# Threshold attention and a bilinear FFN on one core: FFN columns spread over the slots up to the next block, product with v moved by 0.4 of a slot

## The chip, the core and the metric

The kernel runs on one core of a Trainium2 chip. The metric is the device time of one execution in microseconds (us); the kernel before has a median of 1560.83 us over three executions (1559.90, 1560.83 and 1564.76). Everything is in fp32.

## What is computed

Eight batches of eight heads, 576 rows of 64 values each, go through an attention whose weights are kept only where a score is within tau of the maximum of its row. The result, as 4608 tokens of 512 values, goes through a bilinear FFN with 1536 inner columns.

```python
scores = scale * np.matmul(q, k.transpose(0, 1, 3, 2))
thresh = np.max(scores, axis=-1, keepdims=True) - tau
scores = np.where(scores >= thresh, scores, -1000000000.0)
attn = np.exp(scores - np.max(scores, axis=-1, keepdims=True))
attn = attn / (np.sum(attn, axis=-1, keepdims=True) + 1e-09)
attn_out = np.matmul(attn, v)            # (8, 8, 576, 64)
x = attn_out.transpose(0, 2, 1, 3).reshape(4608, 512)
out = ((x @ w_a) * (x @ w_b)) @ w_out    # w_a, w_b: 512 x 1536, w_out: 1536 x 512
```

## The kernel before

**Units and slots.** Two heads of a batch make a pair; there are 32 pairs, four to a batch. The 576 query rows of a pair are cut into four tiles of 128 rows (u = 0 to 3) and a tail of 64 (u = 4, `NT`). A pair and a u are a *unit*, 160 in all. For each batch come first the units u = 0 and 1 of its four pairs, then u = 2, 3 and the tail of each pair (the first batch has an order of its own). The main loop (L632) takes one unit per turn; such a turn, g = 0 to 162, is called a *slot* here. A slot begins on PE with the score matmuls of its unit.

**What a slot issues, in this order.** The program is emitted in one pass, and `keep_order` (L710) fixes on every engine the order in which the instructions were emitted. So where a line stands in the loop decides where its instructions stand in each engine's queue. A slot of the steady part does this:

1. `scores(i, u)` (L640): eight score matmuls into two PSUM buffers `sc` (one for a tail); on DVE a maximum per buffer (L319), on POOL the bias and the threshold (L320, L321).
2. `turn_back` (L641): on SP the load of `wT`, the transposed weights of an earlier unit, out of a scratch tensor `swap` in DRAM; `exchange_blocks` (L642): on POOL eight copies xS<-xT for a block that has become complete.
3. `turn_blocks` of the previous unit (L656): on DVE its transposes (L401, L416), on SP the stores into `swap`.
4. `advance(PORTIONS[0] * pace)` (L658): the first share of the slot's FFN work.
5. `weigh(i, u)` (L660): on ACT the exponential of each `sc` buffer (L332), on DVE the comparison with the threshold (L336), which reads the same `sc` buffer and is its last reader.
6. `prep` (L668): on DVE the transposes of q and k of the next pair; k of a pair is transposed in the slot just before its first scores.
7. `advance(PORTIONS[1] * pace)`, then reciprocal (DVE) and `normalise` (ACT, L355), loads on SP, `advance(PORTIONS[2] * pace)`.
8. If the unit n = g - 3 (`PV_LAG`) completes a part of its pair: `make_room`, then `weighted` (L703), the product with v.
9. `advance(PORTIONS[3] * pace)`.

In the first 15 slots ACT, DVE and POOL also convert the weights of the FFN piece by piece, and the first eight units are turned on PE instead of through DRAM.

**The product with v.** `weighted` (L483) calls `product` (L441), 18 matmuls into one PSUM buffer `pv`, over 256 columns, or over 320 where a part takes in the pair's tail (64 alone for the tails of the first batch). `join` (L437) then adds the two halves of `pv`: a copy of one half on ACT (L438), an addition of the other on DVE (L439); with a tail a second copy and a second addition follow. When the fourth pair of a batch has its part, a *block* of 256 tokens is complete and waits for the FFN.

**The FFN.** `ffn` (L505) is a generator. It works on a block in steps of PE columns: for each of six slices of the inner columns 2048 columns with `w_a` into a PSUM buffer `pab` (emptied by ACT, L536) and 2048 with `w_b` (emptied by DVE, L538), then twice 6144 columns with `w_out` into `po`. A block is 36,864 columns; there are 18 blocks. `advance(cols)` (L575) runs the generator until `cols` columns are used up; when no block is there it returns at once. `make_room` (L596) runs it on until the open PSUM buffer has had at least 1024 columns and has at least 1024 left. `pace`, set at the head of a slot, is 0.09 of a block, plus 576 columns for the product with v, plus 0.05 of what the backlog has above one block; a product takes its columns (5 x 256 or 5 x 320) off what is owed.

**PSUM.** Scores, `pab`, `po` and `pv` share four buffers (`banks`, L122). A buffer is free for the next tile when the last reader of its former tile has been emitted, and the first matmul into it waits for that reader.

After the last slot the remaining blocks run alone (L707).

Of the kernel before, what the change touches and what calls it, by code (L numbers as in the profile page):

```python
# [19 lines left out]
def float_of(bits):  # L20
    return struct.unpack("<f", struct.pack("<I", bits))[0]

PV_LAG = 3
BY_PE = 8
XT_BUFS = 7
W_BUFS = 4
# [3 lines left out]
PACE = 0.09  # L30
CATCH_UP = 0.05
PACE_EARLY = 0.04
ROOM = 1024
PORTIONS = (0.3, 0.4, 0.1, 0.2)


def keep_order(tc):
# [13 lines left out]
def kernel(  # L51
# [37 lines left out]
    B, H, S, D = q.shape  # L89
# [4 lines left out]
    HP = H // 2  # L94
    NT = 4
# [10 lines left out]
    NSLOT = 9  # L106
# [193 lines left out]
    def prep_copy(mT, tp):  # L300
        nc.vector.tensor_copy(mT.rearrange("p (c k) -> p c k", c=2), tp)  # L301
# [82 lines left out]
    def part(i, u):  # L384

        if i < HP:
            return {1: (i, 0), 3: (i, 1), NT: (i, 2)}.get(u)
        return {1: (i, 0), NT: (i, 1)}.get(u)

    def width(i, h):  # L390
        return (HALF, HALF, TAIL)[h] if i < HP else (HALF, HALF + TAIL)[h]
# [45 lines left out]
    def join(out, lo, hi):  # L437
        nc.scalar.copy(out, lo)  # L438
        nc.vector.tensor_tensor(out, out, hi, op=ALU.add)  # L439

    def product(wT, vm, n):  # L441

        pv = banks(n, "pv")
        for s in (NT, 0, 1, 2, 3):
            for r in range(2):
                rows = slice(r * D, (r + 1) * D)
                for j in ((r,) if s == NT else range(2)):
                    k0 = NT if s == NT else 5 * j + s
                    nc.tensor.matmul(pv[j * D:(j + 1) * D, r], vm[rows, k0], wT[rows, k0],  # L449
                                     start=(s == (NT if j == r else 0)), stop=(s == NT - 1))  # L450
        return pv

    def x_tile(name):
        return work.tile([P, HP, HALF], FP32, tag="xT", bufs=XT_BUFS, name=name)

    def exchange(x, xs, hp, c0, c1, engine):

        for r in range(2):
            engine.tensor_copy(xs[r * D:(r + 1) * D, hp, c0:c1], x[(1 - r) * D:(2 - r) * D, hp, c0:c1])  # L459

    def exchange_blocks():
        while complete:
            x, what = complete.pop(0)
            xs = x_tile("xS")
            for hp in range(HP):
                exchange(x, xs, hp, 0, HALF, nc.gpsimd)
            blocks.append(((x, xs), what))
# [15 lines left out]
    def weighted(i, h):  # L483

        b, hp = pairs[i]
        n = width(i, h)
        pv = product(turned.pop((i, h)), loaded[i]["v"], n)
        if h < 2:
            if hp == 0:
                x_of[b, h] = x_tile("xT")  # L490
            lo, hi = (pv[:, r, 0:HALF].rearrange("p (i t e) -> p i t e", t=2, e=Q) for r in range(2))
            join(x_of[b, h][:, hp, :].rearrange("p (t i e) -> p i t e", t=2, e=Q), lo, hi)
            if hp == HP - 1:
                complete.append((x_of.pop((b, h)), ("half", b, h)))
        if n % HALF:
            t = b % GT
            if hp == 0 and t == 0:
                xtail_of[b // GT] = x_tile("xt")
            join(xtail_of[b // GT][:, hp, t * TAIL:(t + 1) * TAIL], pv[:, 0, n - TAIL:n], pv[:, 1, n - TAIL:n])
            del loaded[i], prepared[i]  # L500
            if hp == HP - 1 and t == GT - 1:
                complete.append((xtail_of.pop(b // GT), ("tail", b - t, 0)))
# [69 lines left out]
    BLOCK_COLS = NF * 2 * HP * HALF + 2 * NF * DM  # L572
    running = {"ffn": None, "owed": 0.0, "left": 0, "done": 0, "rest": 0}

    def advance(cols):  # L575
        running["owed"] += cols
        while running["owed"] > 0:
            if running["ffn"] is None:
                if not blocks:
                    running["owed"] = 0.0  # L580
                    return
                running["ffn"] = ffn(*blocks.pop(0))
                running["left"] = BLOCK_COLS
            step, rest = next(running["ffn"], (None, 0))
            if step == 0:
                running["owed"] = 0.0
                return
            if step is None:
                running["ffn"] = None
            else:  # L590
                running["owed"] -= step
                running["left"] -= step
                running["done"] = running["done"] + step if rest else 0
                running["rest"] = rest

    def make_room():  # L596

        while running["rest"] and not (running["done"] >= ROOM and running["rest"] >= ROOM):
            owed = running["owed"]
            running["owed"] = 0.0  # L600
            advance(1)
            running["owed"] += owed - 1

    def backlog():
        return len(blocks) * BLOCK_COLS + (running["left"] if running["ffn"] is not None else 0)
# [3 lines left out]
    units = []  # L609
    for i in range(0, NPR, HP):  # L610
        if i == 0:
            units += [(p, u) for u in (0, 1) for p in range(HP)]
            units += [(p, u) for p in range(HP) for u in (2, 3)]
            units += [(p, NT) for p in range(HP)]
        else:
            units += [(p, u) for p in range(i, i + HP) for u in (0, 1)]
            units += [(p, u) for p in range(i, i + HP) for u in (2, 3, NT)]
    first = {i: g for g, (i, u) in enumerate(units) if u == 0}

    for name in ("q", "k"):  # L620
# [2 lines left out]
    n = 0  # L623
# [4 lines left out]
    def of(g, late):  # L628

        return early.get(g, [])[1:] if late else early.get(g, [])[0:1]  # L630

    for g in range(len(units) + PV_LAG):  # L632
        pace = ((PACE if g > BY_PE else PACE_EARLY) * BLOCK_COLS + (NSLOT + 1) // 2 * S / (NT + 1)
                + CATCH_UP * max(backlog() - BLOCK_COLS, 0))
        written = len(pending)
        here = g < len(units)
        converting = bool(early.get(g)) or bool(early.get(g - 1))
        if here:
            i, u = units[g]
            scores(i, u)  # L640
        turn_back()  # L641
        exchange_blocks()  # L642
        if 2 <= g < BY_PE + 2:
            weighted_unit(*units[g - 2])
            running["owed"] -= (NSLOT + 1) // 2 * P
        for n in of(g - 1, False):
            convert_add(n)
        for n in of(g - 1, True):
            convert_clamp(n)
        if g < 3:  # L650
            prep_copy(*prep_pe(g + 1, "q"))
        for n in of(g - 1, True):
            convert_sign(n)
        load_weights(5 if g < 10 else 4)
        if g > BY_PE and g <= len(units):
            turn_blocks(*units[g - 1])  # L656
        if g > BY_PE:
            advance(PORTIONS[0] * pace)  # L658
        if here:
            weigh(i, u)  # L660
        if 0 < g <= BY_PE:
            turn_pe(*units[g - 1])
        if g < 3:
            prep_copy(*prep_pe(g + 1, "k"))
        for p in range(HP, NPR):
            for name, d in (("q", 2), ("k", 1)):
                if g == first[p] - d:
                    prep(p, name)  # L668
        if g > BY_PE:
            advance(PORTIONS[1] * pace)  # L670
        for n in of(g, False):
            convert_first(n)
            convert_clamp(n)
        if here:
            reciprocal(i, u, nc.scalar if converting else nc.vector)
        for n in of(g - 1, True):
            convert_shift(n)
        for n in of(g - 1, True):
            convert_add(n)
        if here and g < BY_PE:  # L680
            diagonals(i, u)
        elif here:
            normalise(i, u)
        for n in of(g, False):
            convert_sign(n)
        load_weights(5 if g < 10 else 4)
        for p in range(HP, NPR):
            for name, d in (("q", 4), ("k", 3)):
                if g == first[p] - d:
                    load(p, name)  # L690
        for p in range(1, NPR):
            if g == first[p] - 1:
                load_v(p)
        store(written)
        advance((PORTIONS[2] if g > BY_PE else sum(PORTIONS[:3])) * pace)
        for n in of(g, True):
            convert_first(n)
        for n in of(g, False):
            convert_shift(n)
        n = g - PV_LAG  # L700
        if BY_PE <= n < len(units) and part(*units[n]):
            make_room()
            weighted(*part(*units[n]))  # L703
            running["owed"] -= (NSLOT + 1) // 2 * width(*part(*units[n]))
        advance(PORTIONS[3] * pace)
    exchange_blocks()
    while blocks or running["ffn"] is not None:  # L707
# [35 lines left out]
```

## Time and profile before

| what | value |
|---|---|
| median of three executions | 1560.83 us |
| the profiled execution | 1561.63 us |
| its span, first to last instruction | 1559.9 us |
| PE busy | 1490.9 us (96%) |
| DVE busy | 881.9 us (57%) |
| ACT busy | 592.7 us (38%) |
| POOL busy | 260.3 us (17%) |
| mean granted TensorE clock | 0.985 |
| FFN block run alone at the end | 41.4 us `pab` and 20.4 us `po` |

"Busy" is time with an instruction at work; the granted clock is the share of TensorE's pulses that the throttle lets through. In the trace a row "start us, us, engine line op out<-in" is a run of equal instructions; square brackets behind it give the idle time of the engine just before and what ended it. The start of a slot can be read from the first `sc` matmul of its unit: slot 9 begins at 95.3 us, slot 16 at 160.8, slot 30 at 270.4, slot 42 at 366.2, slot 63 at 536.5 and slot 158 at 1354.5.

### The profile page before, as it was taken

Reading aid. Unit: us, or ns where it says so; the run is one execution under the profiler, and the core shown is the slowest. Engines: PE = TensorE matmul, PEld = TensorE weight load, DVE = VectorE, ACT = ScalarE, POOL = GpSimd, SP = SyncE. Lnnn points to the kernel's source line nnn. Section 1 sums busy time; section 2 is a strip of 40 time slices with the busy share of each in tenths; the row PEclk is TensorE's granted clock in tenths of the full one; section 3 lists DMA queues with packets and bytes.
Section 4 is the critical chain, followed back from the end, with each engine's and each line's share of the span. In section 5 each row is a group of like instructions: output and inputs, shape, how many; then the busy total and the mean of one; then the engine's idle time right before and its main releaser. Section 6 shows DMA issues by size and latency. Waiting matters only on the chain.

```text
span 1559.9 us, 51105 instructions
## 1 busy us (share of the span) xinstructions
PE 1490.9 (96%) x22640; PEld 1087.8 (70%) x22640; DVE 881.9 (57%) x1844; ACT 592.7 (38%) x935; POOL 260.3 (17%) x662
## 2 busy tenths in 40 slices
PE   5779999898999999999999999999999999999998
PEld 3666585674768777677867686867686768586775
DVE  5999576465656665675544755466555765510010
ACT  4767344343434443443332443243433443310000
POOL 2666211111111111121100101011110111010000
PEclk8889999998999999999999999999999999999999
DMA  9648887679767886687455965588657976530000
GB/s 202 147 139 225 179 159 166 141 151 193 158 141 169 175 194 142 157 171 179 101 128 117 187 151 140 114 174 180 150 130 140 186 160 140 130 85 16 2 15 15
DMA packets 624558, 220.38 MB, mean 141 GB/s; under 512 B 542929, under 2 KB 612049, under 8 KB 624337
## 3 DMA queue, kind: packets, MB, share of 16 engines
q1 hardware_dynamic: 621968, 216.52, 63.4%
q8 instruction: 178, 2.92, 0.8%
q10 hardware_dynamic: 2368, 0.59, 0.2%
q14 instruction: 44, 0.35, 0.1%
HBM read 127.40 MB, written 89.65 MB: 139 GB/s over the span
## 4 chain that ended last, share of the span: by engine, by line
PE 77%; DVE 8%; DMA 5%; SPq 3%; ACT 2%; issue 2%; POOL 0%; DVEq 0%; POOLq 0%; ACTq 0%
PE pab L530 42%; PE po L550 19%; PE pv L449 8%; PE sc L312 8%; SPq L411 2%; DVE w L336 2%; DMA wT<-swap 2%; DVE mx L319 2%; DMA swap<-tb 2%; DVE low L226 1%; DVE tb L401 1%; SPq L140 1%; DMA qm<-in_q_dram 1%; SPq L423 0%; DMA raw<-in_moe_w_b_dram 0%
## 5 line engine op out<-in xcount | busy, mean ns | idle before, releaser
L550 PE MATMUL po<-wo_sb,h 64*64 64x512 f32 x3456 | 410.1, 590 | 0.0
L332 ACT ACTIVATE w<-sc,bias,scalars 128x576 f32<-128x576 f32 x288 | 228.6, 829 | 237.1 <-POOL bias L320 233.8
L550 PEld LDWEIGHTS po<-wo_sb,h 64*64 64x64 f32 x3456 | 178.8, 133 | 178.9 <-issue 166.5
L319 DVE TENSOR_REDUCE mx<-sc 128x1 f32<-128x576 f32 x288 | 205.8, 751 | 163.8 <-PE sc L312 160.1
L355 ACT ACTIVATE w<-w,rcp 128x576 f32<-128x576 f32 x272 | 197.7, 769 | 234.5 <-DVE rcp L349 234.5
L320 POOL TENSOR_SCALAR bias<-mx,scalars 128x1 f32<-128x1 f32 x288 | 84.8, 294 | 1073.5 <-DVE mx L319 1042.9
L530 PE MATMUL pab<-xS,wa_sb 64*64 64x256 f32 (+1 forms) x3520 | 260.2, 377 | 2.4 <-POOL xS L459 2.4
L312 PE MATMUL sc<-kT,qT 64*64 64x288 f32 x2304 | 239.6, 412 | 21.4 <-DVE kT L301 8.1
L530 PE MATMUL pab<-xS,wb_sb 64*64 64x256 f32 (+1 forms) x3520 | 257.3, 375 | 0.0
L336 DVE SCALAR_TENSOR_TENSOR w<-sc,thr,w 128x576 f32<-128x576 f32 x288 | 222.6, 805 | 18.0 <-ACT w L332 13.8
L530 PE MATMUL pab<-xT,wb_sb 64*64 64x256 f32 (+1 forms) x3136 | 224.2, 378 | 3.2 <-DVE h L538 1.6
L530 PE MATMUL pab<-xT,wa_sb 64*64 64x256 f32 (+1 forms) x3136 | 221.8, 373 | 4.9 <-DVE xT L439 3.5
L530 PEld LDWEIGHTS pab<-xS,wa_sb 64*64 64x64 f32 x3520 | 182.2, 134 | 34.9 <-POOL xS L459 9.0
L530 PEld LDWEIGHTS pab<-xS,wb_sb 64*64 64x64 f32 x3520 | 183.7, 134 | 27.2 <-issue 0.3
L449 PE MATMUL pv<-wT,vm 64*64 64x320 f32 (+3 forms) x2592 | 180.4, 389 | 13.9 <-DMA wT<-swap 13.2
L312 PEld LDWEIGHTS sc<-kT,qT 64*64 64x64 f32 x2304 | 137.5, 134 | 71.7 <-issue 26.2
L530 PEld LDWEIGHTS pab<-xT,wa_sb 64*64 64x64 f32 x3136 | 158.6, 133 | 33.0 <-DVE xT L439 3.8
L530 PEld LDWEIGHTS pab<-xT,wb_sb 64*64 64x64 f32 x3136 | 160.4, 136 | 30.4 <-DVE h L538 2.6
L449 PEld LDWEIGHTS pv<-wT,vm 64*64 64x64 f32 x2592 | 129.8, 136 | 59.9 <-issue 24.5
L401 DVE STREAM_TRANSPOSE tb<-w 128x576 f32<-128x576 f32 x240 | 171.2, 751 | 0.0
L538 DVE TENSOR_TENSOR h<-h,pab 128x512 f32<-128x512 f32 (+1 forms) x110 | 72.6, 660 | 139.3 <-PE pab L530 135.7
L439 DVE TENSOR_TENSOR xT<-xT,pv 128x256 f32<-128x256 f32 (+1 forms) x68 | 27.5, 404 | 208.2 <-ACT xT L438 208.2
(59 smaller groups left out, 769.5 us busy)
## 6 DMA issues: line engine op xcount, KB each, us to landing
swap<-tb SPq DMA_DIRECT2D x240, 288.0 KB, 5.1
wT<-swap SPq DMA_DIRECT2D x28, 1440.0 KB, 7.6
wT<-swap SPq DMA_DIRECT2D x32, 1152.0 KB, 6.2
vm<-in_v_dram SPq DMA_DIRECT2D x32, 288.0 KB, 4.2
swap<-tbt SPq DMA_DIRECT2D x128, 72.0 KB, 2.5
out_dram<-osb SPq DMA_DIRECT2D x32, 256.0 KB, 3.8
qm<-in_q_dram SPq DMA_DIRECT2D x112, 72.0 KB, 3.5
km<-in_k_dram SPq DMA_DIRECT2D x112, 72.0 KB, 4.8
```

The source lines that it names most:

```text
L312: nc.tensor.matmul(sc[j if u < NT else 0][to, c], qT[r, q0:q0 + D], kT[r, c * SH:(c + 1) * SH], start=True, stop=True)
L319: nc.vector.tensor_reduce(mx[:, c], sc[j], axis=AX.XY, op=ALU.max)
L320: nc.gpsimd.tensor_scalar(bias[:, c], mx[:, c], e_nscale, None, op0=ALU.mult)
L332: nc.scalar.activation(w.rearrange("p (c k) -> p c k", c=2), s, AF.Exp, bias=bias[:, j:j + 1], scale=e_scale)
L336: nc.vector.scalar_tensor_tensor(out=wv, in0=s, scalar=thr[:, j:j + 1], in1=wv, op0=ALU.is_ge, op1=ALU.mult, accum_out=sums[:, j:j + 1])
L355: nc.scalar.activation(w, w, AF.Copy, scale=rcp[:, j:j + 1])
L401: nc.vector.transpose(tb[:, j * NB:(j + 1) * NB, (u % 2) * Q:(u % 2 + 1) * Q], w.rearrange("p (n e) -> p n e", e=Q))
L411: nc.sync.dma_start(swap[:, :, g * 2 * Q:(g + 1) * 2 * Q].rearrange("c p w -> p c w"), tb[g * Q:(g + 1) * Q])
L449: nc.tensor.matmul(pv[j * D:(j + 1) * D, r], vm[rows, k0], wT[rows, k0], start=(s == (NT if j == r else 0)), stop=(s == NT - 1))
L530: nc.tensor.matmul(pab[c * D:(c + 1) * D, r], w[rows, f // n, k, fs + c * D:fs + (c + 1) * D], moving, start=(k == 0), stop=(k == H - 1))
L538: nc.vector.tensor_tensor(ht, ht, pab, op=ALU.mult)
L550: nc.tensor.matmul(po[c * D:(c + 1) * D, r], ht[rows, t0:t0 + D], wo_sb[rows, F, :], start=(F == 0), stop=(F == NF - 1))
```

## The change

`PV_LAG` goes from 3 to 4, and the product with v moves from the place behind `advance(PORTIONS[2] ...)` to the one behind `advance(PORTIONS[0] ...)`, ahead of `weigh`. Counted in shares of the FFN work it stood at 0.8 of slot n + 3 and stands now at 0.2 of slot n + 4. The shares go from 0.3, 0.4, 0.1, 0.2 to 0.2, 0.4, 0.2, 0.2. `arrivals` lists the slots in which a new block can be begun, and from slot 9 on the pace is no more than the backlog divided by the number of slots up to the next of them. `pace` is worked out behind the scores instead of ahead of them.

```diff
-PV_LAG = 3
+PV_LAG = 4
-PORTIONS = (0.3, 0.4, 0.1, 0.2)
+PORTIONS = (0.2, 0.4, 0.2, 0.2)
...
+    arrivals = [g + PV_LAG + 1 for g, (i, u) in enumerate(units)
+                if i % HP == HP - 1 and part(i, u) and (i >= HP or u == NT - 1)]
...
     for g in range(len(units) + PV_LAG):
-        pace = ((PACE if g > BY_PE else PACE_EARLY) * BLOCK_COLS + (NSLOT + 1) // 2 * S / (NT + 1)
-                + CATCH_UP * max(backlog() - BLOCK_COLS, 0))
...
         turn_back()
         exchange_blocks()
+        pace = (PACE if g > BY_PE else PACE_EARLY) * BLOCK_COLS
+        if g > BY_PE:
+            pace = min(pace, backlog() / (min([a for a in arrivals if a > g] + [len(units) + PV_LAG + 1]) - g))
+        pace += (NSLOT + 1) // 2 * S / (NT + 1) + CATCH_UP * max(backlog() - BLOCK_COLS, 0)
...
         if g > BY_PE:
             advance(PORTIONS[0] * pace)
+            n = g - PV_LAG
+            if BY_PE <= n < len(units) and part(*units[n]):
+                make_room()
+                weighted(*part(*units[n]))
+                running["owed"] -= (NSLOT + 1) // 2 * width(*part(*units[n]))
         if here:
             weigh(i, u)
...
-        n = g - PV_LAG
-        if BY_PE <= n < len(units) and part(*units[n]):
-            make_room()
-            weighted(*part(*units[n]))
-            running["owed"] -= (NSLOT + 1) // 2 * width(*part(*units[n]))
         advance(PORTIONS[3] * pace)
```

No instruction is added or taken away, and none changes its shape; the engines get the same work in another order.

## Prediction

> **What bounds the kernel now.** I read the page first. Its first part gives PE 96% of the span, the second shows where the other 4% lies:
>
> ```profile
> PE 1490.9 (96%) x22640; PEld 1087.8 (70%) x22640; DVE 881.9 (57%) x1844; ACT 592.7 (38%) x935; POOL 260.3 (17%) x662
> PE   5779999898999999999999999999999999999998
> DVE  5999576465656665675544755466555765510010
> PEclk8889999998999999999999999999999999999999
> ```
>
> Each digit is a fortieth of the span, 39 us. From the fifth on PE is the bound; before that DVE is nearly full too. So time is PE's work plus PE's idle time plus what a throttled clock costs. The windows view, cut at slot borders, sizes this:
>
> ```profile
> core 0: us, PE busy (x) PEld busy (x) DVE busy (x) ACT busy (x) POOL busy (x), PEclk, DMA share, GB/s
> 95.28:160.80 65.52, 57.99 (x1043) 41.83 (x1045) 62.56 (x109) 44.71 (x77) 43.50 (x55) 0.95 0.74 196
> 264.80:291.40 26.60, 20.58 (x234) 12.17 (x232) 13.24 (x29) 9.29 (x14) 5.39 (x16) 0.87 0.74 164
> 359.50:389.90 30.40, 22.98 (x241) 12.31 (x237) 17.38 (x39) 12.10 (x18) 5.68 (x17) 0.83 0.94 204
> 420.30:1390.00 969.70, 964.27 (x14697) 713.49 (x14695) 570.73 (x1234) 376.09 (x566) 127.45 (x414) 1.00 0.70 152
> ```
>
> The first line is slots 9 to 15 (weights converted, DVE busy 62.56 of 65.52 us); the next two are the holes; the last, 970 us, has 5.4 us of idle PE. The PE timeline names the holes:
>
> ```profile
> 270.42 1.17 PE L312 MATMUL sc<-kT,qT 64*64 64x288 f32 x8
> 276.70 3.62 PE L449 MATMUL pv<-wT,vm 64*64 64x256 f32 x34 [5.12 <-DMA wT<-swap]
> 366.17 1.46 PE L312 MATMUL sc<-kT,qT 64*64 64x288 f32 x16
> 373.87 5.00 PE L449 MATMUL pv<-wT,vm 64*64 64x320 f32 x34 [6.23 <-DMA wT<-swap]
> ```
>
> In slots 30 and 42 PE has its scores, no FFN column (the backlog is used up) and then waits for the transposed weights. The products behind these waits take 3.62 and 5.00 us where 2.14 is usual for the first form.
>
> **What the skill says.** "TensorE: Matmul & The Clock Gate", Part 1: an idle window of about 3.4 us halves the clock. The trace agrees: mean clocks of 0.87 and 0.83 around the two holes, 1.00 afterwards; idle times of 1.5 us (largest of the 970 us window) leave it at 1.00. "Perfetto Trace Analysis", Per-instruction lifecycle: "ACT/DVE/GPSIMD are strict FIFO", so an instruction that waits holds all behind it. The trace agrees: the rows below keep the order of emission. "PSUM — Partial Sum Buffer", the section on bank collisions: accesses of two engines to a bank must be kept apart by semaphores. The trace agrees: ACT's second copy out of `pv` starts only after DVE's first addition has ended (538.13 after 538.10).
>
> **The change part by part.** Counting the program's instructions on PE, a column of FFN costs (41.42 + 20.41) / 36,864 = 1.68 ns from the block alone at the end; a slot's scores 0.97 us.
>
> *1. The holes go.* In the changed order every slot from 9 on has FFN columns; slots 30 and 42 get 4096 and 3072 instead of none, and the product is 0.4 slot later. Idle PE that goes: 0.88 and 0.29 us (slots 18, 19), 5.12 and 0.90 (30, 31), 6.23 and 1.19 (42, 43): 14.6. Lost pulses: 26.6 x 0.13 + 30.4 x 0.17 = 8.6, of which 1.0 lies in idle time: 7.6. Gain 22.2 us; bounds 20 and 24. What is late next is part 4.
>
> *2. Thinner early slots.* Slots 9 to 15 lose 3072 of 24,064 columns, 5.2 us of PE work. DVE was busy all but 2.96 us there, so they can't get shorter by more. The columns are done later, where PE is full. Cost between 2.2 and 5.2; I take 4.
>
> *3. A block begun as soon as it is there.* In slots 20, 32 and 44 the first `pab` starts with xT and needs xS within 3 us. POOL's eight copies take 3.57 us and stand behind bias and threshold of the slot's scores (3.3 us after its start). Before, this wait cost 0.29, 0.90 and 1.19 us, counted as gone above. Bounds 0 and 6; I take 3.
>
> *4. The product now stands ahead of the exponential.* This is the step that decides. On ACT the copies of `pv` now come before the slot's two exponentials, on DVE the additions before the two comparisons. Queued behind the waiting copy are: exponentials, comparisons, the transposes of k, and, by PSUM, the scores of the next slot. The end of slot 62 and slot 63 of the kernel before give every duration:
>
> ```profile
> 534.24 2.58 PE L449 MATMUL pv<-wT,vm 64*64 64x320 f32 x33
> 537.27 0.37 ACT L438 COPY xT<-pv 128x256 f32<-128x256 f32 x1 [1.60 <-PE pv L449]
> 537.68 0.42 DVE L439 TENSOR_TENSOR xT<-xT,pv 128x256 f32<-128x256 f32 x1 [1.29 <-ACT xT L438]
> 538.13 0.21 ACT L438 COPY xt<-pv 128x64 f32<-128x64 f32 x1 [0.49 <-DVE xT L439]
> ...
> 539.76 1.55 ACT L332 ACTIVATE w<-sc,bias,scalars 128x576 f32<-128x576 f32 x2 [1.41 <-POOL bias L320]
> 541.20 0.78 DVE L336 SCALAR_TENSOR_TENSOR w<-sc,thr,w 128x576 f32<-128x576 f32 x1
> 541.90 0.81 DVE L336 SCALAR_TENSOR_TENSOR w<-sc,thr,w 128x576 f32<-128x576 f32 x1
> 542.64 0.77 DVE L286 STREAM_TRANSPOSE kT<-km 128x576 f32<-128x576 f32 x1
> 543.56 1.20 PE L312 MATMUL sc<-kT,qT 64*64 64x288 f32 x16 [1.07 <-DVE sums L347]
> ```
>
> The last row shows such a wait already: with only 2560 FFN columns in slot 63, the next scores waited 1.07 us. Over all products (medians) ACT is done with `pv` and can start an exponential 2.81 us after a 256-wide product begins and 4.04 us after a 320-wide one; PE itself goes on after 2.03 and 2.6 us. From the exponential's start the first comparison ends at 0.05 + 0.83 + 0.78 = 1.66, with 0.15 to PE (543.41 to 543.56) 1.8 us; the second at 2.6; a transpose of k behind them at 3.3. Until then the next scores can't begin, if they take the buffer of the first score tile (A), of both (B), or need that k (K). The wait is covered only by FFN columns between the product and the end of the slot: for 256 wide and A (2.81 + 1.8 - 2.03) / 1.68 ns = 1531, and so on. Before, the product stood last and the exponentials began 2.5 to 2.8 us into the slot, so A, B and K were ready at 4.6, 5.4 and 6.1 us, under slots of 5.3 to 11 us.
>
> I took the buffers and columns from the order of the built program for the 54 products of slots 25 to 157:
>
> ```
> width, needs  products  columns needed  short of them  their mean columns  missing, us
> 256, none         5          -               0               -                0
> 256, A            9        1531              2             1024               1.7
> 256, B            7        2006              4             1600               2.7
> 256, K            7        2421              6             1877               5.5
> 320, A           10        1923              9             1024              13.6
> 320, B           10        2398              9             1849               8.3
> 320, K            6        2813              6             1109              17.2
> ```
>
> Sum 49 us in 36 slots. One by hand, slot 57: scores 0.97, 1024 columns 1.72, product begins at 2.7; exponential at 6.74, buffer A ready at 8.5; PE has 2.6 for the product and 1280 columns, 7.45: it waits 1.1 us. Since a wait comes every other or third slot and PE is the bound, nothing takes it back. If each release came 0.5 us sooner the 36 short slots would give up 18 us: 31; if 0.25 us later, 58. I take 49.
>
> *5. The product's own start.* In six slots `pv` takes the buffer of a `pab` that ended in this slot, whose multiplication on DVE (0.67 us) now waits behind two maxima and two transposes of 0.75 us, to about 4.9 us. Against PE's own position 0.6 to 1.4 us are missing each time: 6.4 if all hold, 0 if DVE is ahead. I take 3.
>
> *6. The queues.* The product issues no DMA, but frees `wT` (two buffers) and v. For the tails of the first batch, on SP, three loads of `wT` and the load of v for the fifth pair now wait up to half a slot for it; stores into `swap`, output stores and q and k loads stand behind. Their consumers come two slots later, some 14 us, against 6.2 to 7.6 us for the load from issue to landing: 0, at most 2 if this slack were gone. The later place of the pace's arithmetic costs nothing on the chip.
>
> **The sum.** Against the profiled execution's 1561.6 (span 1559.9 and 1.7 around it; 0.8 above the median): 1561.6 - 22.2 + 4 + 3 + 49 + 3 = 1598.4; on the scale of the median 1597.6, so 1598 us.
>
> **Rivals.** (a) *Faster*: the exponential isn't held long, or the next scores find a free buffer; part 4 shrinks under 10 us, and the time is 1562 - 22 + 4 + 3 + 8 = 1555, or 1545 with nothing of it. Its place is the columns behind each product: were they all above 1531 or 1923, it would win. For it: 96% of busy PE and DVE at 57%, so on average room; against it: the order in the queues is fixed, and slot 63 shows the wait. The sign turns where part 4 falls under 12 us, a quarter of my sum. (b) *No change*: part 4 at 10 to 17 us, 1556 to 1565; the releases would have to come over 0.8 us sooner than the rows say. (c) *Half*: releases 0.5 us sooner or waits partly taken up by PE's order: 31 in part 4, nothing in part 5, 1577. (d) *Worse*: idle times of 3 us and more (slots 43, 103, 123, 143) halve the clock too, 1.7 us each, and parts 3 to 5 are at their upper ends: 1561.6 - 20 + 5 + 6 + 58 + 6 + 7 = 1624. (e) The change doesn't do what it says, and the FFN still runs dry: slots 30 and 42 have columns in the built order, so hardly.
>
> **How the numbers follow.** My forecast (1585 to 1611) 0.55, (c) 0.22, (d) 0.12, (b) and (e) 0.05, (a) 0.06. The range 1574 to 1614 takes in the forecast and (c), and cuts (d) above and (a), (b) below. About 0.3% is what a measurement of this kernel can tell from no change: faster 0.06, same 0.05, slower 0.89.
>
> **What would show it.** In the profile after: no wait of `pv` for `wT` above 1 us and a clock of 1.00 from 200 us on (part 1); PE waiting for DVE ahead of `sc` on L312, some 40 to 50 us in 30 to 40 times, mostly in slots with a 320-wide product (4); ACT idle before its copy from `pv` with exponentials right behind it; waits for POOL before xS in slots 20, 32, 44 (3); `pv` waiting for DVE's h in a few slots (5). I am wrong if L312 waits under 15 us in all.

## The result, and the profile after

Four executions of the changed kernel gave 1583.54 to 1588.27 us, median 1585.24; four of the kernel before on the same chip, median 1561.64. The ratio is 1.0151 with a 95% interval of 1.0127 to 1.0175: slower by 23.6 us. The profiled execution took 1588.27 us, with a span of 1586.5 us.

From the page after, the busy times and three of the rows of forty slices; then two rows of its costliest groups (busy time and mean ns, then the idle time before them and what ended most of it):

```profile
PE 1506.6 (95%) x22640; PEld 1092.4 (69%) x22640; DVE 884.8 (56%) x1844; ACT 586.4 (37%) x935; POOL 262.6 (17%) x662
PE   5779999999999999999999999999999999999998
DVE  5899576667666665565545655565655665520000
PEclk9889999999999999999999999999999999999999
L312 PE MATMUL sc<-kT,qT 64*64 64x288 f32 x2304 | 246.7, 422 | 42.2 <-DVE sums L347 19.9
L438 ACT COPY xT<-pv 128x256 f32<-128x256 f32 (+1 forms) x68 | 24.4, 359 | 316.0 <-PE pv L449 313.2
```

PE still shows nines nearly everywhere and yet the time is longer. DVE, ACT and POOL have the work they had; PE has the same 22,640 matmuls and is "busy" 15.7 us longer (1490.9 before). ACT now stands idle for 313.2 us ahead of its copies out of `pv`, where it was 144.9 before: it stands longer with a waiting copy at the head of its queue. The windows view after, cut at the borders of slots 9 to 15, 30 and 31, 42 and 43, and for the steady part:

```profile
core 0: us, PE busy (x) PEld busy (x) DVE busy (x) ACT busy (x) POOL busy (x), PEclk, DMA share, GB/s
98.37:160.40 62.03, 54.92 (x996) 41.01 (x996) 60.11 (x109) 43.53 (x76) 46.17 (x56) 0.94 0.76 207
266.60:281.00 14.40, 14.40 (x161) 8.20 (x156) 8.16 (x19) 5.25 (x8) 1.40 (x5) 1.00 0.85 185
359.30:374.90 15.60, 13.02 (x147) 6.98 (x139) 11.45 (x25) 6.36 (x11) 1.69 (x6) 1.00 0.97 181
420.30:1420.00 999.70, 979.11 (x14675) 705.48 (x14673) 567.40 (x1215) 368.30 (x560) 126.47 (x408) 0.99 0.67 145
```

The hole in slots 30 and 31 is gone: PE is busy for all of the 14.40 us, at a clock of 1.00. In slots 42 and 43 the clock is 1.00 too, and 2.58 us of idle time are left, of another kind (below). In the steady part the idle time of PE is 20.6 us in 999.7, where it was 5.4 in 969.7. The list of PE's waits from 190 to 1400 us (us in total, times, longest) names it. The kernel before:

```profile
PE pv L449 <- DMA wT<-swap: 12.3, 5, 6.2
PE sc L312 <- DVE sums L347: 4.8, 6, 1.5
```

The changed kernel:

```profile
PE sc L312 <- DVE sums L347: 18.7, 10, 3.0
PE sc L312 <- DVE w L336: 6.7, 13, 0.7
PE pv L449 <- DVE h L538: 2.9, 4, 0.9
...
PE sc L312 <- DVE xt L439: 1.3, 4, 0.6
```

The wait of `pv` for `wT` has left the list. In its place the scores wait for DVE, 26.7 us in 27 times. How that comes about is read in slot 63, the slot that the prediction used; here it begins at 526.87 us. Rows of the timeline (start, length, engine, line, and in brackets the idle time before and its releaser):

```profile
528.70 0.43 PE L449 MATMUL pv<-wT,vm 64*64 64x320 f32 x1
...
530.04 0.28 POOL L320 TENSOR_SCALAR bias<-mx,scalars 128x1 f32<-128x1 f32 x1 [0.30 <-DVE mx L319]
532.07 0.37 ACT L438 COPY xT<-pv 128x256 f32<-128x256 f32 x1 [4.16 <-PE pv L449]
532.47 0.42 DVE L439 TENSOR_TENSOR xT<-xT,pv 128x256 f32<-128x256 f32 x1 [1.19 <-ACT xT L438]
532.93 0.21 ACT L438 COPY xt<-pv 128x64 f32<-128x64 f32 x1 [0.49 <-DVE xT L439]
533.03 1.56 ACT L332 ACTIVATE w<-sc,bias,scalars 128x576 f32<-128x576 f32 x2
533.98 0.82 DVE L336 SCALAR_TENSOR_TENSOR w<-sc,thr,w 128x576 f32<-128x576 f32 x1 [0.58 <-ACT w L332]
534.72 0.81 DVE L336 SCALAR_TENSOR_TENSOR w<-sc,thr,w 128x576 f32<-128x576 f32 x1
535.46 0.77 DVE L286 STREAM_TRANSPOSE kT<-km 128x576 f32<-128x576 f32 x1
536.37 1.20 PE L312 MATMUL sc<-kT,qT 64*64 64x288 f32 x16 [1.77 <-DVE sums L347]
```

Both biases are ready at 530.3 us, and ACT has nothing to do: it has been idle for 4.16 us when its copy starts. The exponentials stand behind that copy in the queue and begin at 533.03, 2.7 us after they could have. Behind them come the comparisons and the transpose of k, which ends at 536.23; the scores of slot 64 start 0.14 us later. The list calls the releaser "sums", the row tells that it was the transpose.

**Where the 26.6 us between the two profiled spans are.** From each slot's length I take its work (0.97 us of scores, 1.68 ns for an FFN column, 2.03 or 2.6 us for a product; columns from the order of the built program). What is left is the slot's excess; "half clock" is what stretches with a granted clock of 0.50 cost:

```
excess, us                                before   after   difference
up to slot 9 (same order on each engine)    63.7    66.8       +3.1
slots 9-15                                  14.2    15.9       +1.7
slots 16-19                                  4.1     1.7       -2.4
slots 30, 31, 42, 43 (the holes)            24.7     3.4      -21.3
all other slots from 20 on                  21.3    66.3      +45.0
  of which half clock after a wait             0    10.2
from slot 159 to the end                   197.1   198.0       +0.9
```

The differences sum to 27.0, not 26.6, because 256 FFN columns (0.4 us of work) that the kernel before does by slot 158 come later in the changed one.

The first row is put down to the execution, not to the change: up to slot 9 the five engines get the same instructions in the same order, and in the profiles of all the kernels here slot 9 begins at 94.9 to 98.4 us, and the profiled executions of the changed kernel and of two below (e2, e5), which are late there, lie 3.0 to 3.8 us above their own medians. Without that row 23.9 us of the table are left, beside 23.6 by the medians. That these executions differ by chance there is likely, but not shown.

### The profile page after: what moved, and what is told of

Same layout as the page of the kernel before. It is cut to its first block, busy times and chain, and to the rows that moved or that the text cites. A ratio compares the mean times of both kernels' runs of the same rounds, so it can differ in the third digit from the quotient of the medians.

```text
span 1586.5 us, 51083 instructions
## 1 busy us (share of the span) xinstructions
PE 1506.6 (95%) x22640; PEld 1092.4 (69%) x22640; DVE 884.8 (56%) x1844; ACT 586.4 (37%) x935; POOL 262.6 (17%) x662
## 4 chain that ended last, share of the span: by engine, by line
PE 81%; DVE 8%; ACT 3%; DMA 3%; SPq 2%; issue 2%; DVEq 0%; POOL 0%; ACTq 0%; POOLq 0%
PE pab L530 41%; PE po L550 21%; PE sc L312 10%; PE pv L449 9%; DVE w L336 2%; ACT w L332 1%; SPq L411 1%; DVE mx L319 1%; DVE low L226 1%; DVE tb L401 1%; DMA raw<-in_moe_w_a_dram 1%; DVE kT L286 1%; DMA raw<-in_moe_w_out_dram 1%; DMA qm<-in_q_dram 0%; PE tp L374 0%
## 5 line engine op out<-in xcount | busy, mean ns | idle before, releaser
L550 PE MATMUL po<-wo_sb,h 64*64 64x512 f32 x3456 | 430.0, 590 | 0.0
L550 PEld LDWEIGHTS po<-wo_sb,h 64*64 64x64 f32 x3456 | 191.5, 133 | 159.6 <-issue 144.6
L312 PE MATMUL sc<-kT,qT 64*64 64x288 f32 x2304 | 246.7, 422 | 42.2 <-DVE sums L347 19.9
L530 PE MATMUL pab<-xS,wb_sb 64*64 64x256 f32 (+1 forms) x3520 | 265.5, 378 | 0.0
L530 PE MATMUL pab<-xS,wa_sb 64*64 64x256 f32 (+1 forms) x3520 | 265.4, 375 | 0.0
L530 PE MATMUL pab<-xT,wa_sb 64*64 64x256 f32 (+1 forms) x3136 | 239.2, 378 | 5.0 <-DVE xT L439 1.8
L530 PE MATMUL pab<-xT,wb_sb 64*64 64x256 f32 (+1 forms) x3136 | 237.9, 377 | 3.7 <-DVE w L336 1.9
L312 PEld LDWEIGHTS sc<-kT,qT 64*64 64x64 f32 x2304 | 130.0, 136 | 121.8 <-issue 48.2
L530 PEld LDWEIGHTS pab<-xT,wa_sb 64*64 64x64 f32 x3136 | 164.6, 135 | 36.3 <-issue 4.9
L438 ACT COPY xT<-pv 128x256 f32<-128x256 f32 (+1 forms) x68 | 24.4, 359 | 316.0 <-PE pv L449 313.2
```

The source lines that it names most:

```text
L312: nc.tensor.matmul(sc[j if u < NT else 0][to, c], qT[r, q0:q0 + D], kT[r, c * SH:(c + 1) * SH], start=True, stop=True)
L530: nc.tensor.matmul(pab[c * D:(c + 1) * D, r], w[rows, f // n, k, fs + c * D:fs + (c + 1) * D], moving, start=(k == 0), stop=(k == H - 1))
L550: nc.tensor.matmul(po[c * D:(c + 1) * D, r], ht[rows, t0:t0 + D], wo_sb[rows, F, :], start=(F == 0), stop=(F == NF - 1))
```

## The experiments

Two theories stood against each other. The one called A in the expectations is part 4 of the prediction: the exponentials and comparisons are held in the queues of ACT and DVE behind the copies and additions of a `pv` that isn't done, and the next scores wait for them. Against it stood that the later product itself (`PV_LAG`, `wT` and v freed later) or the thinner slots cost the time. Each ratio is to the kernel before on the same chip, with its 95% interval; diffs are against the changed kernel unless another is named.

**e1_spread_only.** The product goes back to its old place, one slot earlier; FFN columns stay spread, portions as changed.

```diff
-PV_LAG = 4
+PV_LAG = 3
...
             advance(PORTIONS[0] * pace)
-            n = g - PV_LAG
-            if BY_PE <= n < len(units) and part(*units[n]):
-                make_room()
-                weighted(*part(*units[n]))
-                running["owed"] -= (NSLOT + 1) // 2 * width(*part(*units[n]))
...
+        n = g - PV_LAG
+        if BY_PE <= n < len(units) and part(*units[n]):
+            make_room()
+            weighted(*part(*units[n]))
+            running["owed"] -= (NSLOT + 1) // 2 * width(*part(*units[n]))
         advance(PORTIONS[3] * pace)
```

> The new pace and the new shares alone; the product with v stays behind the third share of slot n + 3. Theory A (the cost comes from the product's copies and additions standing ahead of the slot's exponentials and comparisons; the spreading of the columns pays): the holes of slots 18, 30 and 42 go (some 21 us), the waits of the scores for DVE stay as few as before: 1538 to 1548 us. Theory B (the thinner slots of the spreading cost more than the holes they fill): 1561 us or more.

Measured: 1544.42 us, 0.9889 [0.9871, 0.9908]. Spreading alone is a gain of 17 us: excess in the holes 7.3 us instead of 24.7, in the other slots 19.4. The loss doesn't come from spreading. Slots 9 to 15 are thinner here by 1024 columns only; with the full 3072 fewer, as in the changed kernel, they come in e3.

**e2_move_only.** The other half: the product moved, the old pace and portions.

```diff
-PORTIONS = (0.2, 0.4, 0.2, 0.2)
+PORTIONS = (0.3, 0.4, 0.1, 0.2)
...
-        if g > BY_PE:
-            pace = min(pace, backlog() / (min([a for a in arrivals if a > g] + [len(units) + PV_LAG + 1]) - g))
```

> The product alone moved to 0.2 of slot n + 4; pace and shares as before. Theory A: the waits of the scores for DVE are there as after the change, some 30 us more than before, and the FFN still runs dry; 1585 to 1605 us. Theory B: the move costs nothing and takes the waits for the transposed weights away, 1545 to 1560 us.

Measured: 1612.14 us, 1.0321 [1.0302, 1.0339]. The direction is A's, the size lies above it. The move alone loses 50 us. PE's list of waits over the whole trace of this kernel begins:

```profile
PE sc L312 <- DVE sums L347: 29.1, 12, 4.4
PE sc L312 <- DVE w L336: 14.8, 23, 2.5
```

The excess of the other slots is 90.6 us, and 15.4 us are lost to the clock from 200 us on. Columns that aren't spread would leave some product slots with less cover still, which would explain the size; no run takes that apart.

**e3_weigh_first.** The changed kernel with one thing undone: `weigh` stands ahead of the product. Spreading and the later product remain.

```diff
             advance(PORTIONS[0] * pace)
+        if here:
+            weigh(i, u)
+        if g > BY_PE:
             n = g - PV_LAG
...
-        if here:
-            weigh(i, u)
```

> As after the change, but the slot's exponentials and comparisons are emitted ahead of the product. On PE the product keeps its place; on ACT and DVE its copies and additions come behind. Theory A: the scores no longer wait for DVE beyond what they did before; 1538 to 1550 us. Theory C (it is the product's place on PE, few FFN columns behind it, whatever ACT and DVE do first): within 6 us of the changed kernel, 1579 to 1591 us.

Measured: 1541.66 us, 0.9868 [0.9851, 0.9885], 44 us under the changed kernel by the ratios (0.0283 of 1560). The product has the same place on PE in both kernels and each slot the same FFN columns; what differs is the order of two calls, and that order costs the 44 us. In the trace of this kernel, a product with its slot's exponentials:

```profile
514.58 2.59 PE L449 MATMUL pv<-wT,vm 64*64 64x320 f32 x34
515.20 1.55 ACT L332 ACTIVATE w<-sc,bias,scalars 128x576 f32<-128x576 f32 x2 [1.86 <-POOL bias L320]
516.64 0.78 DVE L336 SCALAR_TENSOR_TENSOR w<-sc,thr,w 128x576 f32<-128x576 f32 x1
517.52 0.37 ACT L438 COPY xT<-pv 128x256 f32<-128x256 f32 x1 [0.76 <-PE pv L449]
518.09 0.42 DVE L439 TENSOR_TENSOR xT<-xT,pv 128x256 f32<-128x256 f32 x1
519.89 1.20 PE L312 MATMUL sc<-kT,qT 64*64 64x288 f32 x16
```

The exponentials run while PE works on the product (514.58 to 517.17), the copy waits 0.76 us, and the next scores have no bracket. PE's waits of 190 to 1400 us:

```profile
PE pv L449 <- DMA wT<-swap: 3.3, 3, 1.5
PE pv L449 <- DVE h L538: 3.3, 5, 0.8
PE sc L312 <- DVE sums L347: 3.1, 4, 1.0
```

**e4_k_earlier.** In the changed kernel q and k of the next pair are transposed, and loaded, a slot earlier: the next scores then can wait for their buffer, but not for k.

```diff
-            for name, d in (("q", 2), ("k", 1)):
+            for name, d in (("q", 3), ("k", 2)):
...
-            for name, d in (("q", 4), ("k", 3)):
+            for name, d in (("q", 5), ("k", 4)):
```

> As after the change, but q and k of a pair are loaded and transposed one slot earlier, so that no scores wait for a transpose of k that stands behind delayed comparisons. Theory A: the twelve waits of that kind shrink from some 23 us to 10, and the halved clock behind the four longest of them (some 9 us) goes: 1560 to 1568 us. Theory D (the comparisons alone set these waits, the transpose of k is covered): 1580 to 1588 us.

Measured: 1566.15 us in 20 executions, 1.0031 [1.0023, 1.0039]; 19 us of the 24 come back. "sums" is gone from the list, here of the whole trace; what is left for `sc` are waits for buffers, from 190 us on 10.0 us in 19 times, none above 0.7:

```profile
PE sc L312 <- DVE w L336: 14.0, 23, 2.5
```

No half clock is left from 200 us on, where the changed kernel loses 10.2 us to it: the long waits, those with half clock behind them, were those for k.

**e5_before_k_earlier.** The same edit in the kernel before.

> The kernel before, with q and k of a pair loaded and transposed one slot earlier. If the kernel before already paid about 10 us for scores that wait behind a transpose of k, in the slots where the changed kernel waits for it too (which the sum of the prediction did not take off), it is at 1549 to 1554 us. If those waits are of the comparisons alone, it stays at 1558 to 1563 us.

Measured: 1555.44 us in ten executions, 0.9969 [0.9958, 0.998], between the two expectations. The kernel before had lost some 5 us to late transposes of k already (4.8 by the ratio, 5.7 by the medians). A quarter to a third of what e4 gained is thus no loss of the change.

**e6_wf_early_full.** e3 with slots 9 to 15 at the old pace, for the price of part 2.

```diff
-        if g > BY_PE:
+        if g > 15:
             pace = min(pace, backlog() / (min([a for a in arrivals if a > g] + [len(units) + PV_LAG + 1]) - g))
```

> As the run with the exponentials ahead of the product (1541.7 us), with the new pace from slot 16 on only, so that slots 9 to 15 keep their full columns. If thinner early slots cost 2 to 5 us, as predicted: 1536 to 1540 us. If DVE's own work sets these slots and the columns can as well be done later: 1540 to 1544 us.

Measured: 1542.84 us, 0.9884 [0.9867, 0.99]: no gain over e3 (0.9868). The columns put early aren't saved: the excess of slots 9 to 15 falls from 16.7 to 14.0 us, that of slots 16 to 19 rises from 0.4 to 3.8, nearly all of it in slot 19, which has only 512 FFN columns left instead of 2048.

**e7_wf_k_earlier.** e3 and the edit of e4 together.

> As the run with the exponentials ahead of the product (1541.7 us), with q and k of a pair loaded and transposed one slot earlier. Where that run still waits for DVE behind a transpose of k (3 us in 4 waits by its trace): 1536 to 1540 us. If the wait only moves to the comparisons: 1541 to 1543 us.

Measured: 1536.18 us, 0.9844 [0.9824, 0.9863], the best version found, under both kernels. Between 190 and 1400 us the list has no wait of L312; its first entry is a product's wait for its buffer:

```profile
PE pv L449 <- DVE h L538: 3.2, 5, 0.9
```

**e8_portion_04.** The changed kernel with the product put 0.2 of a slot further back, so that fewer columns come behind it.

```diff
-PORTIONS = (0.2, 0.4, 0.2, 0.2)
+PORTIONS = (0.4, 0.2, 0.2, 0.2)
```

> As after the change, with shares of 0.4, 0.2, 0.2, 0.2: the product comes a fifth of the slot's columns later (some 740 columns, 1.2 us), still ahead of the exponentials. Theory A: every product with too few columns behind it loses 1.2 us more and others begin to lose, 40 to 60 us in all: 1625 to 1650 us. If the waits are not set by what lies between the product and the slot's end: 1580 to 1595 us.

Measured: 1643.17 us, 1.0524 [1.0508, 1.0539], another 58 us. PE's waits of 190 to 1400 us:

```profile
PE sc L312 <- DVE sums L347: 37.8, 14, 4.3
PE sc L312 <- DVE w L336: 15.0, 25, 1.0
PE sc L312 <- DVE xt L439: 6.9, 10, 1.5
```

The columns between the product and the next scores are the cover, as part 4 says; 20.5 us are lost to the clock besides.

**e9_exp_first.** Which queue costs the time? `weigh` is cut in two: the exponentials go ahead of the product, the comparisons (`compare`) stay behind it. ACT isn't held then, DVE is. Seven lines added ahead of L347 make it L354.

```diff
             ws.append(w)
+        exped[i, u] = (sc, thr, sums, ws)
+
+    def compare(i, u):
+
+        sc, thr, sums, ws = exped.pop((i, u))
         for j, s in enumerate(sc):
...
             advance(PORTIONS[0] * pace)
+        if here:
+            weigh(i, u)
+        if g > BY_PE:
             n = g - PV_LAG
...
         if here:
-            weigh(i, u)
+            compare(i, u)
```

> As after the change, but the exponentials are emitted ahead of the product and only the comparisons stay behind it: ACT's queue is free, on DVE the additions still stand before the comparisons. By the rows the first score buffer is then free 0.42 us (256 wide) or 0.60 us (320 wide) sooner; the sum of the waits falls by a third, about 16 us, and most of the halved clock behind the longest goes, up to 9 us: 1560 to 1571 us. If only ACT's queue matters: 1540 to 1548 us. If only DVE's does: 1580 to 1588 us.

Measured: 1563.58 us in 20 executions, 1.0018 [1.0009, 1.0027]. By the ratios the order on DVE costs 23 us by itself (1.0018 against 0.9868), and the order on ACT another 21 on top of it (1.0151 against 1.0018). What ACT's order would cost alone isn't known: comparisons need their exponentials, and no run holds ACT without DVE. From 190 us on the scores wait for k, and besides only 1.3 us for `xt`:

```profile
PE sc L312 <- DVE sums L354: 12.8, 8, 2.4
```

**e10_move_weigh_first.** e2 with `weigh` ahead of the product: the later product alone, without spreading and without holding.

> The product at 0.2 of slot n + 4 with the exponentials and comparisons ahead of it, and the pace and shares of the kernel before: what the later product is worth alone, without the delay and without the spreading. If the holes are of empty FFN slots and only the spreading fills them: 1552 to 1562 us. If the later product alone takes the waits away: 1540 to 1547 us.

Measured: 1550.40 us, 0.9937 [0.992, 0.9953], between the two expectations. The later product alone gains 10 us, and no wait of `pv` for `wT` is left in its list from 190 to 1400 us (12.3 us before); spreading adds another 11 (e3), and the two overlap, since spreading alone has 17 (e1). Without spreading, holding costs 60 us (1.0321 less 0.9937), with it 44.

**e11_wf_portion_04** and **e12_wf_k_portion_04.** The portions of e8 in e3 and in e7: does the later place inside the slot cost anything by itself?

> Exponentials and comparisons ahead of the product, and shares of 0.4, 0.2, 0.2, 0.2: the control to the run that put the product a fifth of a slot later and took 1643 us. Theory A: with the exponentials ahead the product's place costs nothing, 1536 to 1545 us. If a later product with fewer columns behind it costs by itself: 1580 us or more.

> The same with q and k of a pair one slot earlier, as in the run of 1536.2 us. There the product waits in six slots, 4 us in all, for DVE's multiplication whose buffer it takes; later in the slot DVE is through with it: 1530 to 1536 us. If that wait only moves behind the product: 1536 to 1540 us.

Measured: e11 1550.43 us, 0.9937 [0.9922, 0.9953]; e12 1537.42 us, 0.9858 [0.984, 0.9877]. With `weigh` ahead the step from 0.2 to 0.4 costs 11 us by the ratios, not 58; with k earlier as well nothing that the intervals can tell from zero. e11 missed A's range by 5 us, and e12 lies in the second of its ranges: in its list the wait for DVE's multiplication falls from 3.2 to 1.7 us, without a gain in time. The trace of e11 still shows waits for k:

```profile
PE sc L312 <- DVE sums L347: 11.5, 8, 2.3
```

These 8 waits are gone in e12. The excess of e11 over e3, about 8 us, lies in slots 9 to 15 (3.0), 16 to 19 (1.3), the holes (1.6) and the rest (3.0), less 0.8 ahead of slot 9. Some 5 us of it are half clock: in slots 9 to 15 the mean granted clock is 0.90 (e3: 0.95), 3.4 us more lost, and e11 loses 1.7 us more behind a wait at 876 us. Why its clock falls more often in slots 9 to 15 stays open.

## Why the prediction was right, and where its sum was not

The forecast of 1598 us was 13 us too high, the result inside its range. The mechanism was right; that the total came so near is partly luck: part 4 with part 5 was 22 us too dear, and half clock that the forecast left out took 10 of them back. The sum in the prediction's own steps, on the scale of the profiled executions:

```
part                                  forecast   measured by slots
1  holes go                             -22.2        -23.7
2  thinner slots 9-15                    +4           +1.7
3  slots 20, 32, 44                      +3           +4.6
4, 5  exponentials held, pv for h       +52          +30
   half clock after waits                 0          +10
   end; start of slot 9                   0           +0.9; +3.1
sum                                     +36.8        +26.6
```

(Rounded, and without the 0.4 us of columns named above.)

*Part 1 held.* Slots 16 to 19 fell by 2.4 and the holes by 21.3 us; e1 confirms the gain apart from the move. The 3.4 us of excess that the holes' slots still have are part 4: 2.63 us of it the wait of slot 44's scores.

*Part 2 was a little too dear.* DVE was busy 60.11 of 62.03 us, so the slots did get shorter, by 3.5 us for 5.2 us of columns. e6 shows that the question was put wrongly: the columns are in short supply up to slot 19, and where they go among these slots decides nothing.

*Part 3 was right in two slots of three.* The three slots have 4.6 us of excess, about none before. PE's rows of slots 20, 32 and 44:

```profile
192.92 1.96 PE L530 MATMUL pab<-xT,wa_sb 64*64 64x256 f32 x32 [1.33 <-DVE osb L439]
285.01 3.64 PE L530 MATMUL pab<-xS,wa_sb 64*64 64x256 f32 x30
379.38 3.01 PE L530 MATMUL pab<-xS,wa_sb 64*64 64x256 f32 x30
```

In slots 32 and 44 the first pass over xS takes 3.64 and 3.01 us where the pass over xT in the first row takes 1.96: its weight loads wait for POOL's copies one after the other, 3.2 us in all. In slot 20 nothing waits for xS; there PE waited 1.33 us for DVE's addition out of a `po` buffer, which the prediction hadn't named. So xS costs about the 3 us that were forecast, and the rest of the 4.6 is something else. None of it is part 4: e3, where nothing is held, has 4.7 us of excess in these slots.

*Part 4 was right in its mechanism, product by product.* e3 (0.9868 against 1.0151) shows it, e8 its cover, and e9 that DVE's order costs by itself and ACT's adds to it. ACT can start an exponential 2.81 us after a 256-wide product begins, as before, and mostly 4.04 to 4.47 after a 320-wide one, where the forecast had 4.04. Single slots, forecast (worked out from its table) against excess, which can shift by some 0.15 us with where a slot's border is set: slot 60 1.51 and 1.51 us, slot 63 2.15 and 2.24, slot 120 1.95 and 2.05, slot 140 1.95 and 1.95, slot 57 1.08 and 0.93. By class:

```
width, needs     forecast   after    before
256, none          1.4       0.7      -
256, A             1.7       2.6      -
256, B             4.1       1.6      -
256, K             6.9       4.5      2.1
320, A            14.2      13.1      2.3
320, B            10.0       8.2      1.6
320, K            17.2      17.5     10.7
sum               55.5      48.3
```

(Forecast with part 5 at its upper end; the column after without the clock's share; of the 10.7 before, 4.7 are slot 43's and so the holes'; where no figure stands it was small.)

*The term that was mis-sized: part 4 took the whole wait for its cost.* In the same slots the kernel before had paid 12.4 us already, the holes' slots left out. The prediction showed one such wait itself (1.07 us ahead of the scores of slot 64) and yet added the whole wait after the change. e5 says the same from the other side: some 5 us of the waits for k were there before. From 55.5 this leaves 55.5 - 12.4 = 43; another 7 us are missing over the classes, mostly in those that need B, and 3.4 lie in the holes' slots and are counted there: 32, beside the 30 that the slots give as a whole. Why the 7 us are missing isn't settled. The result is near the 31 of rival (c), but not for its reason: no release came 0.5 us sooner.

*The term left out: the clock.* The forecast expected "a clock of 1.00 from 200 us on". The prediction put half clock into rival (d), at 7 us with a chance of 0.12, though it named slots 43, 103, 123 and 143 as having idle times of 3 us and more itself. It came behind the waits that end slots 25, 103, 123 and 143 and cost 10.2 us. Windows of the changed kernel, columns as above:

```profile
234.05:237.46 3.41, 1.48 (x24) 0.97 (x24) 2.29 (x7) 1.49 (x3) 0.00 (x0) 1.00 0.93 168
237.46:240.87 3.41, 3.41 (x37) 2.58 (x32) 3.36 (x5) 2.41 (x4) 0.84 (x3) 0.50 0.48 84
240.87:244.29 3.42, 3.42 (x68) 2.90 (x64) 1.79 (x7) 0.62 (x1) 0.00 (x0) 1.00 0.64 182
370.57:373.99 3.42, 1.75 (x14) 0.40 (x6) 2.08 (x5) 2.04 (x4) 0.00 (x0) 1.00 0.83 142
373.99:377.40 3.41, 2.45 (x32) 1.50 (x36) 2.24 (x7) 1.44 (x2) 0.29 (x1) 1.00 0.87 218
698.25:701.67 3.42, 1.53 (x24) 0.81 (x24) 3.00 (x8) 1.50 (x3) 0.00 (x0) 1.00 0.82 212
701.67:705.08 3.41, 3.41 (x40) 1.20 (x33) 3.33 (x5) 2.06 (x3) 1.92 (x6) 1.00 1.19 241
1073.72:1077.13 3.41, 1.16 (x16) 0.54 (x8) 2.24 (x7) 1.95 (x4) 0.00 (x0) 1.00 0.88 239
1077.13:1083.96 6.83, 6.03 (x56) 3.89 (x60) 4.66 (x9) 2.99 (x4) 2.32 (x7) 0.50 0.72 155
```

In the second and the last row the clock is 0.50, and PE counts as nearly fully busy while its matmuls take longer: 37 of them in 3.41 us in the second row, 68 in the third. One such stretch lasts 3.41 or 6.83 us and costs half of that, 1.7 or 3.4 us; the four together 10.2. What these borders have to do with it is said at the end.

*Part 5 and 6.* `pv` waits for DVE's h 2.9 us in four products (forecast 3 in six). From 190 to 1400 us no engine is listed as waiting for a load or a store: 0, as said.

*What would show it.* The 40 to 50 us of waits on L312 in 30 to 40 times came as 26.7 us in 27 from 190 us on (18.7, 6.7 and 1.3 above), over the 15 us under which the prediction would have been wrong, also when the 4.8 us of before are taken off. The list falls short of the excess. The Trainium skill, "Perfetto Trace Analysis", in its Per-instruction lifecycle, says that the profiler estimates the end of a TensorE instruction and doesn't observe it. The trace fits that: PE is busy 15.7 us longer for the same instructions, of which half clock can make at most 10.2, and the listed idle time of slot 57 is 0.65 us where the slot is 0.93 too long. So some of a wait seems to be counted as busy; no run here separates it.

*The rivals.* (a) and (b) fall with the interval, which begins at 1.0127. Their mechanism, a place for the exponentials that isn't held, is real, but had to be made (e3: 0.9868). (d) had the clock right and its sizes not. (e) falls: the holes are gone. Two of the prediction's figures are off by little: with nothing of part 4 rival (a) sums to 1547, not 1545, and from the durations as printed the columns needed come out 5 to 13 higher than in its table, under 0.03 us each.

Open: why slot 9 begins up to 3.5 us later in some executions (all those with k transposed earlier are among them); why e11's clock falls more often in slots 9 to 15; and the 7 us by which the classes fell short.

## What to carry to other kernels

Where each engine works in the order of emission, moving a producer (here the product on PE) also moves its consumers on the other engines; put work whose data are ready, above all work that releases PE's next buffer, ahead of an instruction that waits for PE. When such a wait is priced, count per place only what is new: take off what the same place waits already, and add the clock for each wait of 2 us and more (here 1.7 or 3.4 us for each time it was halved). And two halves of a change can have opposite signs (here -17 and +50 us, and +24 together): run them apart before the whole is judged.

## What the runs showed of the hardware that was not expected

The granted clock changes on a fixed grid of 3.41 us. In each of the 14 profiles all its changes lie on multiples of 3.413 us from one another, within 3 ns; where the grid lies differs from run to run. Cut at these borders, the windows above explain what the waits alone don't. The wait of 2.63 us that ends at 374.95 us is longer than that of 1.93 us which ends at 236.27; but the border at 373.99 divides it, so that PE is idle for 1.67 us in one window and 0.96 in the next, and the clock stays at 1.00. The 1.93 us lie in one window, and the next has half clock. The 1.89 us of the window at 698.25 were not enough.

Over the 14 profiles, from 200 to 1400 us, the window behind one with at least 2.0 us of listed idle PE had half clock 28 times in 28; behind 1.65 to 2.0 us 6 times in 13; behind less 7 times in 307, four of them behind a window that had half clock itself; and never in 4574 behind a window with under 0.05 us of idle time. No reason is known for the other three (one in e1, two in the holes of the kernel before).

The Trainium skill, "TensorE: Matmul & The Clock Gate", Part 1, has the window of 3413 ns, free-running, and the trace agrees. It ties the half clock to an idle window. Here the measurement differs: some 2 us of listed idle time in one window were enough, as in the four windows of the changed kernel (1.93, 2.62, 2.25 and 1.90 us). What it costs is plain: 10.2 us in the changed kernel, 20.5 in e8, nothing from 200 us on in e3, e4 and e7.
